# Fixed rings, a first sequence in halves, decays on C and their inverse on x, and weights that GpSimd's DMA queue casts on the way

## The chip, the cores and the metric

The kernel runs on one core of a Trainium2 chip. A core has TensorE (PE, matrix products), VectorE (DVE), ScalarE (ACT), GpSimd (POOL) and SyncE (SP), which all work from lists of instructions in order, and 16 DMA engines. Here only SyncE, ScalarE and GpSimd issue DMAs. The metric is the device time of one execution in microseconds: median 124.69 us of three runs (124.38 to 125.62) for the kernel before.

## The reference

A state-space scan (four batches called sequences here, eight heads, 768 steps, head dimension 32, state dimension 16) is followed by a two-layer network with a GELU on the 3072 tokens of 256 features. Cut to what matters:

```
log_a = log(clip(a, 1e-6, 1))
for each chunk c (32 steps here; any chunk length gives the same y):
    cum = cumsum(log_a[c])
    M   = (C_c B_c^T) * exp(cum_i - cum_j) * causal
    y_c = M x_c + (C_c state) * exp(cum_i)
    state = exp(sum log_a[c]) * state + B_c^T (x_c * exp(cum_last - cum_j))
x   = y as [tokens, heads * head_dim]           # 3072 x 256
out = gelu_tanh(x @ w_in) @ w_out               # w_in 256 x 2048, w_out 2048 x 256
```

All inputs and the output are float32. Both kernels keep products of decays instead of logarithms and multiply bf16 on TensorE.

## The kernel before

**Work.** Chunks of 128 steps: six per sequence, 24 in all, in units of one chunk (units 0 and 1) or two (units 2 to 12). For a unit, `f_G` makes the grams C B^T of all heads into the bank tile `gb` (L648), `f_M` masks them into `m` (L658, VectorE), `f_D` makes the state's increments (L669), `f_S` and `f_SP` update the state and spread it by head (L719, L726, VectorE), `f_Y` makes the output into `yb` (L691, L700), and `f_yev` copies it to `xm` (L709, ScalarE). Then the network: `f_s1` is a group of eight or four matmuls with w_in (L746) into one of two banks `hp`, `f_gelu` turns a bank into `gT` (L754, ScalarE, 96 times), `f_s2` is a group of four matmuls with w_out (L763) into one bank, and `f_oev` and `f_store` take a chunk out (L770, L772). The last chunk goes in two halves of columns (`f_s2h`, L781).

**Sequence preparation.** The decays' products run backwards through a chunk (`f_R`, `f_scang`); B is multiplied by them and C by their reciprocal, then both are transposed: chunk 0 by a path of its own (`f_mul0`, `f_T0`, `f_ce0`, `f_bh0`), the rest of sequence 0 by TensorE (`f_RT`, L481; `f_mul`, L584; `f_T`, L593; `f_E`; `f_F`, L608), sequences 1 to 3 on VectorE (`f_mulg`, L522; `f_Tg`, L532; `f_Fg`, L542). B in its plain layout, which `f_D` needs, comes by transposing back on TensorE (`f_N`, L614) and a copy on ScalarE (`f_bn`, L447). x is cast to bf16 by `f_castx` (L449 on GpSimd).

**Weights.** w_in and w_out come in four quarters each, as float32, through SyncE's queue (`load_wi` L439, `load_wo` L443) into tiles `wf`; `f_wi` and `f_wo` cast them into `w_in_sb` and `w_out_sb` (L449 GpSimd, L451 VectorE).

**Order.** Every step is a node with an engine, a duration, dependencies and a priority. `run_order` plays the nodes and emits them in the order of its own clock; the table `PRIO` holds the priorities. The loads take places in SyncE's list in the order in which the code names them: B and C, x, w_in, x, w_in, x, w_out, x, then the sequences. Where TensorE would be idle before the first `f_s2`, `idle` puts in matmuls on zeros (fillers, L1054).

Of the kernel before, what the change touches and what calls it, by code (L numbers as in the profile page):

```python
# [14 lines left out]
class Node:  # L15


    def __init__(self, eng, dur, fn, deps=(), prio=0.0, done=0.0):
        self.eng, self.dur, self.fn, self.prio, self.done = eng, dur, fn, prio, done
        self.deps = [d for d in deps if d is not None]  # L20
        self.allocs = []
        self.after = 0.0
        self.start = self.end = None

    def takes(self, pool, *by):

        self.allocs.append((pool, list(by)))
        return self


def run_order(nodes, pools, hop=0.08, same=0.04, idle=None, wait=()):

    hist = {p: [] for p in pools}
    free = {}
    todo = list(nodes)
    order = []

    def est(n):
        t = 0.0
        for d in n.deps:  # L40
            if d.end is None:
                return None
            t = max(t, d.end + n.after
                    + (d.done + hop if d.eng != n.eng else 0.0 if n.eng == "PE" else same))
        for pool, _ in n.allocs:
            h = hist[pool]
            if len(h) >= pools[pool]:
                for d in h[-pools[pool]]:
                    if d.end is None:
                        return None  # L50
                    t = max(t, d.end + (same if d.eng == n.eng else hop))
        return t

    while todo:
        best = None
        cand = {}
        for n in todo:
            e = est(n)
            if e is not None:
                cand.setdefault(n.eng, []).append((e, n))  # L60
        assert cand, [(n.eng, n.prio, n.fn) for n in todo[:5]]
        for eng, c in cand.items():
            t = max(free.get(eng, 0.0), min(e for e, _ in c))
            if best is None or t < best[0]:
                best = (t, eng)
        t, eng = best
        ready = [(n.prio, e, i, n) for i, (e, n) in enumerate(cand[eng]) if e <= t + 1e-9]
        ready.sort(key=lambda r: r[:3])
        n = ready[0][3]
        if eng in wait:  # L70
            soon = [(e, m) for e, m in cand[eng] if t < e < t + n.dur - 0.1 and m.prio < n.prio - 5]
            if soon:
                e1 = min(e for e, _ in soon)
                fit = [r[3] for r in ready if t + r[3].dur <= e1 + 0.1]
                if fit:
                    n = fit[0]
                else:
                    t, n = min(((e, m) for e, m in soon if e <= e1 + 0.1),
                               key=lambda r: r[1].prio)
        if idle is not None and eng == "PE":  # L80
            x = idle(free.get(eng, 0.0), t)
            if x is not None:
                order.append((free.get(eng, 0.0), x))
        n.start, n.end = t, t + n.dur
        free[eng] = n.end
        for pool, by in n.allocs:
            hist[pool].append(by)
        todo.remove(n)
        order.append((t, n.fn))
    return order  # L90
# [1001 lines left out]
```

## Time and profile before

| | |
|---|---|
| median of three runs | 124.69 us (124.38 to 125.62) |
| span of the profiled execution, first to last instruction | 122.2 us |
| what lies around the span (median less span) | 2.5 us |
| first `f_s1` group | starts 12.30 us |
| last cast of a w_out quarter | 24.86 us, 1.04 us long |
| last matmul's end | about 118.8 us |

The profile is of one execution; its own time outside of the profiler isn't shown, so its span is set beside the median of the runs. Busy shares of the page are averages over the whole span. A matmul's entry lasts longer than the slot it takes in the pipeline: groups of eight with 256 columns follow each other 0.87 us apart, 0.109 us each.

### The profile page before, as it was taken

What the parts mean: (1) busy time and instruction counts of PE and PEld (TensorE: products, weight loads), DVE (VectorE), ACT (ScalarE), POOL (GpSimd) and SP (SyncE); (2) the same over time, 40 slices, a digit from 0 to 9 for tenths busy, and PEclk for the clock granted to TensorE, in tenths of its full rate; (3) what the DMA queues carried; (4) which work ended last, traced back from release to release, by engine and by line L of the source; (5) the groups of instructions that cost most, each with busy time, mean ns of one, the idle gap of its engine ahead of it and who ended that gap; (6) DMA issues with size and microseconds to landing.
All of it is one profiled execution on the core that took longest, in us unless ns stands there. A gap on an engine that the chain in (4) does not pass through costs nothing.

```text
span 122.2 us, 3518 instructions
## 1 busy us (share of the span) xinstructions
PE 112.5 (92%) x1484; PEld 98.9 (81%) x1484; DVE 69.7 (57%) x161; ACT 75.8 (62%) x145; POOL 18.7 (15%) x38
## 2 busy tenths in 40 slices
PE   5899969999999999779997799999999999999980
PEld 5788658788988898678986679989898899999970
DVE  3887888929979997961959549065656300000100
ACT  4024836775765877468675566768677867767710
POOL 7304565560050005003200000000000000000000
PEclk9999999999999999999999999999999999999999
DMA  2999939979958796598011010111011001111111
GB/s 51 255 267 244 343 106 353 326 163 192 201 151 217 141 222 167 148 197 205 6 43 43 5 43 0 48 46 43 5 43 43 27 21 43 43 48 43 38 48 43
DMA packets 44250, 14.27 MB, mean 117 GB/s; under 512 B 39052, under 2 KB 42700, under 8 KB 44236
## 3 DMA queue, kind: packets, MB, share of 16 engines
q1 hardware_dynamic: 43148, 13.95, 46.1%
q10 hardware_dynamic: 1088, 0.11, 0.7%
q8 instruction: 11, 0.18, 0.6%
q14 instruction: 3, 0.02, 0.1%
HBM read 10.91 MB, written 3.15 MB: 115 GB/s over the span
## 4 chain that ended last, share of the span: by engine, by line
PE 73%; SPq 13%; DMA 5%; ACT 4%; issue 1%; POOL 1%; DVE 0%; ACTq 0%; DVEq 0%
PE hp L746 31%; PE o_ps L763 30%; SPq L431 5%; DMA wf<-in_moe_w_out_dram 5%; SPq L443 4%; PE yb L763 3%; ACT gT L754 2%; PE gb L648 2%; SPq L439 2%; PE yb L700 2%; PE yb L691 2%; PE gb L781 1%; SPq L315 1%; ACT o_sb L770 1%; POOL w_out_sb L449 1%
## 5 line engine op out<-in xcount | busy, mean ns | idle before, releaser
L754 ACT ACTIVATE gT<-hp 128x512 bf16<-128x512 f32 x96 | 54.1, 596 | 24.9 <-PE hp L746 24.7
L746 PE MATMUL hp<-xm,w_in_sb 128*128 128x256 bf16 (+1 forms) x416 | 53.6, 267 | 4.0 <-ACT gT L754 2.7
L746 PEld LDWEIGHTS <-w_in_sb 128*128 128x128 bf16 x416 | 42.0, 115 | 7.9 <-issue 5.7
L763 PE MATMUL o_ps<-w_out_sb,gT 128*128 128x256 bf16 x336 | 44.4, 273 | 0.5 <-POOL w_out_sb L449 0.5
L763 PEld LDWEIGHTS <-gT 128*128 128x128 bf16 x368 | 35.7, 98 | 4.3 <-issue 0.7
L658 DVE TENSOR_TENSOR m<-gb,tri 128x1024 bf16<-128x1024 f32 (+1 forms) x25 | 28.5, 1174 | 1.0 <-PE gb L648 1.0
L772 DVE COPY o_sb<-o_ps 128x256 f32<-128x256 f32 x1 | 0.4, 424 | 18.6 <-ACT gT L754 18.6
L770 ACT ACTIVATE o_sb<-o_ps 128x256 f32<-128x256 f32 x20 | 7.7, 385 | 5.0 <-ACT gT L754 2.6
L719 DVE SCALAR_TENSOR_TENSOR s_new<-s_new,pend,hp 128x64 f32<-128x64 f32 x16 | 4.5, 279 | 11.0 <-PE hp L669 10.8
L726 DVE SCALAR_TENSOR_TENSOR sp_new<-s_new,pend,bmask 128x256 bf16<-128x256 f32 x20 | 10.2, 521 | 0.3
L1054 PE MATMUL o_ps<-wz 128*128 128x128 bf16 x75 | 8.9, 281 | 1.3 <-DVE warm L353 1.3
L449 POOL CAST x<-xs_t 128x512 bf16<-128x512 f32 x9 | 5.4, 635 | 26.5 <-DMA xs_t<-in_x_dram 17.3
L709 ACT ACTIVATE xm<-yb 128x512 bf16<-128x512 f32 (+1 forms) x13 | 7.3, 563 | 2.3 <-PE yb L700 2.1
L1054 PEld LDWEIGHTS <-wz 128*128 128x128 bf16 x75 | 6.9, 129 | 1.6 <-DVE warm L353 1.3
L700 PE MATMUL yb<-m,x 128*32 128x128 bf16 x192 | 6.3, 223 | 0.0
L449 POOL CAST w_in_sb<-wf 128x512 bf16<-128x512 f32 x6 | 4.3, 728 | 8.9 <-DMA wf<-in_moe_w_in_dram 8.9
L691 PE MATMUL yb<-ce,sp_new 128*32 128x128 bf16 x160 | 5.3, 221 | 0.0
L648 PE MATMUL gb<-ce,bh 32*128 32x256 bf16 x96 | 5.1, 278 | 0.0
L717 DVE COPY s_new<-hp 128x64 f32<-128x64 f32 x4 | 0.9, 221 | 7.0 <-PE hp L669 7.0
L449 POOL CAST w_out_sb<-wf 128x1024 bf16<-128x1024 f32 x4 | 4.2, 1041 | 3.0 <-DMA wf<-in_moe_w_out_dram 3.0
L700 PEld LDWEIGHTS <-x 128*32 128x32 bf16 x192 | 3.8, 97 | 0.8 <-issue 0.8
L691 PEld LDWEIGHTS <-sp_new 128*32 128x32 bf16 x160 | 2.9, 96 | 1.7 <-issue 1.6
(83 smaller groups left out, 69.5 us busy)
## 6 DMA issues: line engine op xcount, KB each, us to landing
out_dram<-o_sb SPq DMA_DIRECT2D x23, 128.0 KB, 1.7
xs_t<-in_x_dram SPq DMA_DIRECT2D x3, 768.0 KB, 5.9
wf<-in_moe_w_in_dram SPq DMA_DIRECT2D x4, 512.0 KB, 8.8
wf<-in_moe_w_out_dram SPq DMA_DIRECT2D x4, 512.0 KB, 6.9
bc_t<-in_B_dram SPq DMA_DIRECT2D x12, 96.0 KB, 3.1
bc_t<-in_C_dram SPq DMA_DIRECT2D x12, 96.0 KB, 2.3
x_t<-in_x_dram SPq DMA_DIRECT2D x6, 128.0 KB, 7.3
bc_t<-in_C_dram SPq DMA_DIRECT2D x1, 384.0 KB
```

What stands on the lines that cost most here:

```text
L449: nc.gpsimd.tensor_copy(out=o, in_=i)
L648: nc.tensor.matmul(out=gb[:, g, 256 * k:256 * k + 256], lhsT=bh_of(gc)[32 * g:32 * g + 32], rhs=ce_of(gc)[32 * g:32 * g + 32], start=True, ...
L658: nc.vector.tensor_tensor(out=MT[gc][:, g0:g1], in0=gb[:, g0:g1, 256 * k:256 * k + 256] .rearrange("p g (e t) -> p g e t", e=2), in1=tri_b ...
L691: nc.tensor.matmul(out=y4[32 * j:32 * j + 32, k, w], lhsT=sp[:, 32 * h:32 * h + 32], rhs=ce_of(gc)[:, h % 2], start=first(j), stop=False, ...
L700: nc.tensor.matmul(out=y4[32 * j:32 * j + 32, k, w], lhsT=X16[u][:, k, 32 * h:32 * h + 32], rhs=m[:, h // 2, h % 2, :], start=first(j), st ...
L709: nc.scalar.activation(xm[:, :, t0:t0 + n * Q].rearrange("p w (c t) -> p c w t", c=n), y4[:, 0:n], AF.Copy)
L726: nc.vector.scalar_tensor_tensor(out=sp_new.rearrange("p (g d) -> p g d", g=4), in0=state[("s", gc)].rearrange("p (o d) -> p o d", o=1).to ...
L746: nc.tensor.matmul(out=hp[:, j * nt:(j + 1) * nt], lhsT=w_in5[:, kc, fi // 4, fi % 4], rhs=xm[:, kc, t0:t0 + nt], start=(kc == 0), stop=(k ...
L754: nc.scalar.activation(gts[u][:, i * per:(i + 1) * per, 0:nt], hps.pop((u, i)).rearrange("p (j t) -> p j t", j=per), AF.Gelu_apprx_tanh)
L763: nc.tensor.matmul(out=ops[gc], lhsT=gts[u][:, fi, tt * Q:(tt + 1) * Q], rhs=w_out_sb[:, fi, :], start=(fi == 0), stop=(fi == NF - 1), ski ...
L770: nc.scalar.activation(o_sb, ops.pop(gc), AF.Copy)
L1054: nc.tensor.matmul(out=zb[:, 0:128], lhsT=wz[:, 0:128], rhs=wz[:, 0:128], start=True, stop=True)
```

## The change

The scheduler with its nodes and priorities goes. In its place stands a string `ORDER` of 630 words, each a step with its arguments, which is played from the front; it sets each engine's list. Tile pools become single tiles and rings that hand out their buffers in turn. The beginning of the string, which covers the steps up to chunk 0's `f_s2`:

```
c,wz c,cz c,idf c,tri c,ident lbc,0,0,SP la,1,ACT la,3,ACT la,0,SP la,2,ACT c,first c,selp c,aone
bz,0,0,3,DVE lbc,0,1,SP lbc,1,0,SP clip lbc,1,1,SP c,warm bz,0,3,6,POOL lx,0,SP dwi,0 lx,1,SP scan
z,19,g T,0,2 E,0,2,0,43,ACT z,5,g N,0,1 E,0,2,43,64,ACT bn,0,1,ACT p6 cz,0,1 lx,3,SP lx,2,SP pt,0
N,1,3 bn,1,3,ACT bz,1,3,6,ACT pt,2 cz,0,0 T,0,1 E,0,1,0,43,ACT inv,0,0,1 cz,1,1 cz,1,0 c,m16
bz,1,0,3,POOL e2,0 e2,1 T,0,0 E,0,0,0,43,ACT c,bmask pp E,0,1,43,64,ACT asp G,0 E,0,0,43,64,DVE
M,0,0,0,2 M,0,0,2,4 T,1,0 E,1,0,0,64,ACT pend xs,0,POOL T,1,1 E,1,1,0,64,ACT dwi,1 pt,1 inv,0,1,6
T,1,2 D,0 G,1 Y,0 E,1,2,0,64,ACT yev,0 xs,1,POOL z,2,o N,3,6 bn,3,6,ACT S,0,0 M,1,0,0,4 s1,0,0 SP,0
D,1 dwi,2 G,2 S,1,0 xs,2,POOL Y,1 ge,0,0 pk dwi,3 dwo,0 dwo,1 z,11,o s1,0,1 dwo,2 dwo,3 ge,0,1
...
```

`dwi` and `dwo` are the weights, `xs` the scaling of x, `s1`, `ge` and `s2` the network, `z` fillers, `lbn` and `cbn` B in its plain layout, `l...` loads. What else changes:

- **Weights**: one DMA for each quarter, issued by GpSimd, from float32 in memory into the bf16 tile. No cast instruction is left.
- **Decays**: the products run forwards (`f_scan`, `f_scang`); C is multiplied by them, B is only cast, and x is multiplied by their inverse (`f_inv`, `f_xs`) where it was only cast before. The sign of heads is put in by two zero-filled tiles `cz` for sequence 0.
- **Sequence 0** comes in two halves of 384 steps on 64 partitions each; chunk 0 has no path of its own any more. The end-of-chunk decays go through GpSimd (`f_e2`, `f_pend`).
- **Sequences 1 to 3**: B in its plain layout is loaded a second time, 64 bytes at a time (`f_lbn`), and cast on GpSimd (`f_cbn`); the transposing back and its copy go. B's cast is on GpSimd too (`f_cB`). Their loads have buffers of their own.
- **Outputs**: seven whole chunks are taken out by VectorE instead of one.
- Gram, increment and output of a unit are single steps, where before they went as one from unit 5 on. There are five `gT` buffers, six before.

```diff
-    def load_wi(q):
-        WF[("i", q)] = wfp.tile([128, 2, 512], FP32, name="wf")
-        nc.sync.dma_start(out=WF[("i", q)], in_=wi[:, :, q * 512:(q + 1) * 512])
...
-    def f_wi(q, k0, k1, eng):
-        for k in range(k0, k1):
-            copy(eng, w_in_sb[:, k, q * 512:(q + 1) * 512], WF[("i", q)][:, k])
...
+    def f_dwi(q):
+        nc.gpsimd.dma_start(out=w_in_sb[:, :, q * 512:(q + 1) * 512], in_=wi[:, :, q * 512:(q + 1) * 512])
+
+    def f_dwo(q):
+        nc.gpsimd.dma_start(out=w_out_sb[:, 4 * q:4 * q + 4], in_=wo[q])
...
+    def f_lbn(b, q):
+        queue[q].dma_start(out=bnf[b], in_=bass.AP(
+            tensor=B.tensor, offset=B.offset + b * H * S * N, ap=[[N, Q], [Q * N, H * CPB], [1, N]]))
...
+    def f_inv(b, c0, c1):
+        js = slice(H * b, H * b + H)
+        nc.vector.reciprocal(invp[:, c0:c1, js], (pk if b else ptok)[:, c0:c1, js])
...
+    def f_cz(half, e):
+        s = slice(64 * half, 64 * half + 64)
+        nc.vector.tensor_tensor(
+            out=cz[e][s].rearrange("p r (g e) n -> p e r g n", e=2)[:, e],
+            in0=bc0[s, 1].rearrange("p (g e) (r n) -> p e r g n", e=2, n=N)[:, e],
+            in1=p6[s, :, 0:H].rearrange("p r (g e o) -> p e r g o", e=2, o=1)[:, e]
+            .to_broadcast([64, R6, 4, N]), op=ALU.mult)
...
+    def f_cbn(b, eng):
+        copy(eng, bn[b].rearrange("p c (h n) -> p c h n", n=N),
+             bnf[b].rearrange("p (h c) n -> p c h n", c=CPB))
...
+    def f_xs(u, eng):
+        n = len(UNITS[u])
+        X16[u] = x16.take()
+        b, c = divmod(UNITS[u][0], CPB)
+        o = X16[u][:, 0:n].rearrange("p c (h d) -> p c h d", h=H)
+        w = invp[:, c:c + n, H * b:H * b + H].rearrange("p c (h o) -> p c h o", o=1)
+        if b:
+            ttt(eng, o, xs[b].rearrange("p (h c) d -> p c h d", c=CPB)[:, c:c + n],
+                w.to_broadcast([128, n, H, D]))
+        else:
+            for k in range(n):
+                ttt(eng, o[:, k], XT[c + k], w[:, k].to_broadcast([128, H, D]))
...
+    steps = {k[2:]: f for k, f in locals().items() if k.startswith("f_")}
+    for word in ORDER.split():
+        name, *args = word.split(",")
+        steps[name](*(int(v) if v.isdigit() else v for v in args))
```

More of the change, by code (lines that the diff above doesn't have):

```diff
@@ L10 @@
 BF16 = mybir.dt.bfloat16
+I32 = mybir.dt.int32
 AF = mybir.ActivationFunctionType
 ALU = mybir.AluOpType
[L15 to L28, printed above, removed]
@@ L31, in run_order @@
[L31 to L90, printed above, removed]
@@ L251, with __init__, take @@
+s1,12,7 ge,12,6 s2,12,0,1,y ge,12,7 s2,12,0,2,y s2,12,0,3,y s2h,0 s2h,1 oev,21,ACT oev,22,DVE
+oevh,0,DVE st,22 sth,0 st,21 oevh,1,ACT sth,1
+"""
+class Ring:
+    def __init__(self, bufs):
+        self.bufs, self.n = bufs, 0
+    def take(self):
+        self.n += 1
+        return self.bufs[(self.n - 1) % len(self.bufs)]
 @with_exitstack
@@ new lines @@
+    a_t = sb("a_t", [128, 256])
+    ac = sb("ac", [128, 256])
+    p_t = sb("p_t", [128, 256])
+    first = sb("first", [128, 256])
+    p6 = sb("p6", [128, R6, BH])
+    pk = sb("pk", [128, CPB, BH])
+    invp = sb("invp", [128, CPB, BH])
+    e2 = sb("e2", [128, 2, batch, 2, 3])
+    asp = sb("asp", [128, 2, batch, CPB])
+    pend = sb("pend", [128, batch, CPB])
+    ptok = ob[:, 0:CPB * BH].rearrange("p (c j) -> p c j", c=CPB)
+    ptok3 = ob[:, 0:CPB * BH].rearrange("p (k l j) -> p k l j", k=2, l=3)
@@ new lines @@
+    warm = sb("warm", [128, 1])
+    idf = sb("idf", [128, 128])
+    ident = sb("ident", [128, 128], BF16)
+    bmask = sb("bmask", [128, H * D], BF16)
+    tri = sb("tri", [128, Q], BF16)
+    tri_b = tri.rearrange("p (o q t) -> p o q t", o=1, q=1).to_broadcast([128, 4, 2, Q])
+    sel8 = sb("sel8", [128, H])
+    selp = sb("selp", [128, H, N])
+    m16 = sb("m16", [128, 16])
+    par = sb("par", [128, 2])
+    pari = sb("pari", [128, 2], I32)
+    zeros = wz.bitcast(FP32)
+    XT, X16, MT, DT, ST, SP, GT, HP, OP, OS, PT = ({} for _ in range(11))
@@ L451, in copy, with ttt @@
             nc.vector.tensor_copy(out=o, in_=i)
-    def f_wi(q, k0, k1, eng):
-        for k in range(k0, k1):
-            copy(eng, w_in_sb[:, k, q * 512:(q + 1) * 512], WF[("i", q)][:, k])
-    def f_wo(q, eng):
-        copy(eng, w_out_sb[:, 4 * q:4 * q + 4], WF[("o", q)])
-    def f_clip(i0, i1):
-        nc.vector.tensor_scalar(out=ac[:, i0:i1], in0=a_t[:, i0:i1], scalar1=1e-6, scalar2=1.0,
+    def ttt(eng, o, i0, i1, op=ALU.mult):
+        (nc.gpsimd if eng == "POOL" else nc.vector).tensor_tensor(out=o, in0=i0, in1=i1, op=op)
@@ new lines, with f_la, f_lbc @@
+    queue = {"SP": nc.sync, "ACT": nc.scalar, "POOL": nc.gpsimd}
+    def f_la(k, q):
+        t0 = 192 * k - 64 * (k % 2)
+        c0, n = (0, 256) if k % 2 else (64, 192)
+        queue[q].dma_start(out=a_t[32 * k:32 * k + 32, c0:c0 + n], in_=bass.AP(
+            tensor=a.tensor, offset=a.offset + t0, ap=[[S, BH], [1, n]]))
+    def f_lbc(i, half, q):
+        src = (B, C)[i]
+        queue[q].dma_start(
+            out=bc0[64 * half:64 * half + 64, i],
+            in_=bass.AP(tensor=src.tensor, offset=src.offset + half * HS * N,
+                        ap=[[R6 * N, 64], [S * N, H], [1, R6 * N]]))
@@ L485, in f_recip0, with f_p6, f_pt @@
-    def f_recip0():
-        nc.vector.reciprocal(q0, rp0)
-    def f_recip():
-        nc.vector.reciprocal(pt, RP[1])
+    def f_p6():
+        nc.vector.transpose(out=p6, in_=p_t[:, 64:256].rearrange("q (p r) -> q r p", r=R6))
+    def f_pt(l):
+        k, off = (0, 64) if l == 0 else (1, 128 * (l - 1))
+        nc.tensor.matmul(out=ptok3[:, :, l], lhsT=p_t[:, off:off + Q],
+                         rhs=idf.rearrange("p (k o j) -> p o k j", k=2, o=2)[:, k],
+                         start=True, stop=True, skip_group_check=True)
@@ new lines, in f_pp, with f_asp, f_pend @@
+    def f_pp():
+        nc.tensor.matmul(out=pps, lhsT=selp.rearrange("p h n -> p (h n)"),
+                         rhs=e2.rearrange("p t b k l -> p (t b k l)"), start=True, stop=True,
+                         skip_group_check=True)
+    def f_asp():
+        nc.scalar.activation(asp.rearrange("p t b c -> p (t b c)"), pps, AF.Copy)
+    def f_pend():
+        nc.gpsimd.tensor_tensor(out=pend[:, :, 0:CPB - 1], in0=asp[:, 1, :, 0:CPB - 1],
+                                in1=asp[:, 0, :, 1:CPB], op=ALU.mult)
@@ new lines, in f_T, with f_E @@
+    def f_T(half, w):
+        s = slice(64 * half, 64 * half + 64)
+        src = bz if w == 2 else cz[w]
+        t = yb if (half == 0 and w == 0) else hp.take()
+        PT[(half, w)] = t[:, 0:HS // 2].bitcast(BF16)
+        for r in range(R6):
+            nc.tensor.transpose(out=PT[(half, w)][:, r * 64:(r + 1) * 64],
+                                in_=src[s, r].rearrange("p h n -> p (h n)"), identity=ident[s, s])
+    def f_E(half, w, p0, p1, eng):
+        o = bh[0] if w == 2 else ce[0][:, w]
+        copy(eng, o[:, HS * half:HS * half + HS].rearrange("q (p r) -> q p r", r=R6)[:, p0:p1],
+             PT[(half, w)].rearrange("q (r p) -> q p r", r=R6)[:, p0:p1])
@@ L491, in f_clipg, with f_N, f_bn @@
+    def f_N(c0, c1):
+        PT[("n", c0)] = hp.take()[:, 0:HS].bitcast(BF16)
+        for c in range(c0, c1):
+            nc.tensor.transpose(out=PT[("n", c0)][:, c * Q:(c + 1) * Q],
+                                in_=bh[0][:, c * Q:(c + 1) * Q], identity=ident)
+    def f_bn(c0, c1, eng):
+        copy(eng, bn[0][:, c0:c1].rearrange("p c n -> p (c n)"), PT[("n", c0)][:, c0 * Q:c1 * Q])
     def f_clipg(b):
-        nc.vector.tensor_scalar(out=ac3[b], in0=at[b], scalar1=1e-6, scalar2=1.0,
+        nc.vector.tensor_scalar(out=at[b], in0=at[b], scalar1=1e-6, scalar2=1.0,
@@ L553, in f_pp @@
-    def f_pp():
-        RP[2] = psh.tile([128, 512], FP32, name="hp")
-        nc.tensor.matmul(out=RP[2][:, 0:NCH], lhsT=selp.rearrange("p h n -> p (h n)"),
-                         rhs=pe2.rearrange("p j c -> p (j c)"), start=True, stop=True,
-                         skip_group_check=True)
-    def f_pend():
-        nc.scalar.activation(pend.rearrange("p (b i c) -> p i b c", b=batch, i=2),
-                             RP[2][:, 0:NCH].rearrange("p (i b c) -> p i b c", b=batch, i=2), AF.Copy)
@@ L611, in f_N @@
-    def f_N(b):
-        U[b]["n"] = (gb[:, 1] if b else psh.tile([128, 512], FP32, name="hp"))[:, 0:S // 2].bitcast(BF16)
-        for c in range(1 if b == 0 else 0, CPB):
-            nc.tensor.transpose(out=U[b]["n"][:, c * 128:(c + 1) * 128],
-                                in_=U[b]["bh"][:, c * Q:(c + 1) * Q], identity=ident)
-    def f_bn(b, eng):
-        d = U[b]
-        d["bn"] = work.tile([128, CPB, 128], BF16, name="bn")
-        c0 = 1 if b == 0 else 0
-        copy(eng, d["bn"][:, c0:].rearrange("p c n -> p (c n)"), d["n"][:, c0 * 128:])
@@ L656, in f_M @@
         if g0 == 0:
-            MT[gc] = msb.tile([128, 4, 2, Q], BF16, name="m")
+            MT[gc] = mr.take()
         nc.vector.tensor_tensor(out=MT[gc][:, g0:g1],
@@ L738, in f_s1 @@
         per = 512 // nt
-        if u not in gts:
-            gts[u] = gpool.tile([128, NF, 256], BF16, name="gT")
-        hp = psh.tile([128, 512], FP32, name="hp")
-        hps[(u, i)] = hp
+        if u not in GT:
+            GT[u] = gtr.take()
+        HP[(u, i)] = hp.take()
         for j in range(per):
@@ L767, in f_oev, with f_st @@
     def f_oev(gc, eng):
-        o_sb = opool.tile([128, d_model], FP32, name="o_sb")
-        if eng == "ACT":
-            nc.scalar.activation(o_sb, ops.pop(gc), AF.Copy)
-        else:
-            nc.vector.tensor_copy(out=o_sb, in_=ops.pop(gc))
-        outs[gc] = o_sb
-    def f_store(gc):
-        nc.sync.dma_start(out=out[gc * Q:(gc + 1) * Q, :], in_=outs.pop(gc))
+        OS[gc] = orr.take()
+        copy(eng, OS[gc], OP[gc])
+    def f_st(gc):
+        nc.sync.dma_start(out=out[gc * Q:(gc + 1) * Q, :], in_=OS[gc])
     def f_s2h(h):
         for f in range(NF):
-            nc.tensor.matmul(out=gb[:, 2 * h, 0:128], lhsT=gts[NU - 1][:, f, Q:2 * Q],
+            nc.tensor.matmul(out=gb[:, 2 * h, 0:128], lhsT=GT[NU - 1][:, f, Q:2 * Q],
                              rhs=w_out_sb[:, f, 128 * h:128 * h + 128], start=(f == 0),
@@ L785, in f_oevh, with f_sth @@
     def f_oevh(h, eng):
[L786 to L789 removed]
+        OS[("h", h)] = orr.take()
+        copy(eng, OS[("h", h)][:, 0:128], gb[:, 2 * h, 0:128])
+    def f_sth(h):
         nc.sync.dma_start(out=out[(NCH - 1) * Q:NCH * Q, 128 * h:128 * h + 128],
[L791 to L803 removed]
@@ L1036 @@
-    for u in range(MERGE, NU):
-        Yn[u].deps.append(gpn[(u - 2, 0)])
-    for u in range(GT_BUFS, NU):
-        gpn[(u, 0)].deps.append(oevn[UNITS[u - GT_BUFS][-1]])
-    for n in nodes:
-        n.prio = PRIO.get(n.name, n.prio)
-    zb = pso.tile([128, 512], FP32, name="o_ps")
-    def idle(t0, t1):
-        t0 = max(t0, 1.25)
-        n = int((t1 - t0 - 0.05) / (0.107 if t0 < 6.3 else 0.2 if 9.5 < t0 < 13.2 else 0.07))
-        if s2_first[0].start is not None or n < 1:
-            return None
-        def fill():
-            for _ in range(n):
-                nc.tensor.matmul(out=zb[:, 0:128], lhsT=wz[:, 0:128], rhs=wz[:, 0:128],
-                                 start=True, stop=True)
-        return fill
@@ L1058, with f_z @@
-    pools = {"hp": 2, "o": 1, "gram": 1, "yb": 1, "wf": 6, "ob": 6}
-    order = run_order(nodes, pools, idle=idle, wait=("DVE", "POOL"))
-    for t, fn in order:
-        fn()
+                          in_=OS[("h", h)][:, 0:128])
+    def f_z(n, bank):
+        t = gb[:, 3] if bank == "g" else ob
+        for _ in range(n):
+            nc.tensor.matmul(out=t[:, 384:512], lhsT=wz[:, 0:128], rhs=wz[:, 0:128],
+                             start=True, stop=True)
+    steps = {k[2:]: f for k, f in locals().items() if k.startswith("f_")}
```

757 lines of the change are left out of this document (256 added, 501 removed), and 152 rows, old and new, of the table PRIO.

## The prediction

> **What bounds the kernel now.** I read the page first (busy time, slices, chain), then busy time by stretch, then the order of time of the first 26 us, then the rows of the tile `wf`.
>
> ```profile
> span 122.2 us, 3518 instructions
> PE 112.5 (92%) x1484; PEld 98.9 (81%) x1484; DVE 69.7 (57%) x161; ACT 75.8 (62%) x145; POOL 18.7 (15%) x38
> PE 73%; SPq 13%; DMA 5%; ACT 4%; issue 1%; POOL 1%; DVE 0%; ACTq 0%; DVEq 0%
> ```
>
> TensorE (PE) is 73% of the chain that ended last; the 13% of SyncE's queue and the 5% of DMA all lie at its start. Busy time by stretch (columns: length, then busy us and count of PE, PEld, DVE, ACT, POOL, clock, DMA share, GB/s) shows where PE is not full:
>
> ```profile
> 16.00:20.00 4.00, 3.21 (x60) 3.07 (x60) 3.65 (x6) 1.91 (x5) 2.50 (x4) 1.00 0.61 229
> 24.68:49.00 24.32, 24.32 (x328) 21.06 (x328) 19.41 (x49) 16.88 (x33) 5.32 (x8) 1.00 0.90 183
> 49.00:53.00 4.00, 2.63 (x23) 2.22 (x22) 3.90 (x12) 2.18 (x4) 0.00 (x0) 1.00 0.68 151
> 65.00:72.00 7.00, 5.50 (x83) 4.43 (x80) 4.11 (x11) 4.26 (x9) 0.00 (x0) 1.00 0.09 30
> 72.00:118.80 46.80, 46.74 (x582) 42.61 (x574) 15.09 (x26) 31.96 (x62) 0.00 (x0) 1.00 0.11 37
> ```
>
> From 24.68 on PE is full but for two short stretches; the chain has 4.2 us on ScalarE (ACT) there (0.61+0.39+0.61 near 50, 0.38+0.61+0.61+0.39+0.61 from 65 to 72), where one bank waits to be emptied. So the kernel is a **ramp** up to about 25 us and a **full PE** after it. The order of time shows the ramp:
>
> ```profile
> 1.25 2.74 PE L1054 MATMUL o_ps<-wz 128*128 128x128 bf16 x24 [1.25 <-DVE warm L353]
> ...
> 9.71 1.33 POOL L449 CAST w_in_sb<-wf 128x512 bf16<-128x512 f32 x2 [5.52 <-DMA wf<-in_moe_w_in_dram]
> ...
> 12.30 0.95 PE L746 MATMUL hp<-xm,w_in_sb 128*128 128x128 bf16 x8
> ...
> 13.94 0.61 PE L746 MATMUL hp<-xm,w_in_sb 128*128 128x128 bf16 x8
> ...
> 24.68 0.60 PE L763 MATMUL o_ps<-w_out_sb,gT 128*128 128x256 bf16 x4 [0.51 <-POOL w_out_sb L449]
> ...
> 25.98 0.60 PE L763 MATMUL o_ps<-w_out_sb,gT 128*128 128x256 bf16 x4
> ```
>
> The first w_in quarter is cast at 9.71, the first `f_s1` group (L746) runs at 12.30, and the third and fourth quarters of w_out let chunk 0's last two `f_s2` groups (L763) go at 24.68 and 25.98. I take 25.98 as the **marker**: by then 12 `f_s1` groups are done (64 matmuls of 128 columns, 16 of 256), and 118.76-25.98 = 92.8 us of PE follow. Before it PE runs fillers (L1054).
>
> **The change, part by part.**
>
> *Weights.* Eight cast pieces go from GpSimd (4.3 + 4.2 us in the costliest groups) and two from VectorE (0.9). On GpSimd all of that was hidden except where it was last, at 24.68. In exchange the eight loads stand in GpSimd's own order, and they stand late: the second after the scaling of x for chunk 0, the third after chunk 1's, the fourth after chunks 2 and 3's. The changed program's list of instructions with their waits shows more. The first `f_s1` group's second weight load waits for the second w_in transfer, though it needs the first alone; the third w_in transfer waits for that group's last matmul; the second `f_s1` group waits for the third and the fourth transfer. (A transfer now writes both halves of `w_in_sb` at once, where each cast wrote one; the dependence is kept for the whole span between.) So there is a loop: transfer 2, `f_s1` group 1, transfer 3, x scaling, transfer 4, `f_s1` group 2. I follow it:
> - GpSimd up to transfer 2. Constants until 2.3 (like before's 1.69, with a wider `idf` and `tri` moved ahead). The copy of B's first half waits for its load: issued at 0.80, before's rows for B and C of the same tensors land after 3.2 to 4.8 us, the lower as the queues are empty: 4.0. Copy 0.6 (CAST 128x256 0.585). Issue 1. `m16` 0.12+0.18+0.26. Second copy 0.6: 6.8. Four tiny multiplications at 0.2: 7.6. `bmask` 0.31+0.45+0.45: 8.9. `pend` 0.2: 9.1. x scaling 0.65 (no two-input row of GpSimd; 0.585 is a one-input cast of that size): **issue of transfer 2 at 9.8**.
> - A GpSimd DMA issue isn't in this trace. SyncE's issues took 0.36 to 1.64 us when not stuck in a queue; I take 1.0, keep 0.4 to 1.6.
> - Landing. The only row for such a load is
>
> ```profile
> DMA to landing us min/median/max: 4.2/7.0/9.4
> ```
>
> and lower still by the 1.7 us of a 128 KB store, plus 1.3 us for the other 384 KB at 300 GB/s: 3.0. I take 5.0, near the row's minimum, since the weights have a queue of their own but share the 16 engines with x, B, C and sequence 1's loads, which SyncE can now issue at once (no buffer holds them back); both ends, 3.0 and 7.0, are kept.
> - Transfer 2 lands 14.8; group 1 done 15.6; transfer 3 issued 15.6 to 16.6; two x scalings 1.3: 17.9; transfer 4 lands **22.9**, when group 2 starts (before: 13.94). The w_out loads are issued right behind and land by 27, ahead of their use.
> - From there to the marker the new order has 10 `f_s1` groups, 3 of `f_s2`, the grams and outputs of unit 2. PE: 13 x 0.437 + 1.06 + 12 fillers at 0.055 = 7.4; the gelus at 0.60 with two banks: 6.6 with one eviction. PE decides: 7.4. But PE stood almost idle from about 11 to 22.9, and this trace has a half-speed state: 24 fillers at 114 ns each at 1.25, eight L746 in 0.95 at 12.30 and the same eight in 0.61 at 13.94 (about 0.10 and 0.055 apiece), with the clock row at 1.00 all along. I count 3.3 us of wall time at half speed: +1.6. Marker at 22.9 + 9.0 = **31.9**: +5.9 us, with one `f_s1` group still to do (+0.44).
>
> The Trainium skill (TensorE: Matmul & The Clock Gate, Part 1) has that as a gate: PE idle for a window of about 3.4 us falls to half rate and needs about as much activity to come back. The trace agrees with the two rates, not with the clock row. By that rule the sum is the one above; without it 1.6 less.
>
> The Trainium skill (DMA: Bandwidth & Descriptors, Anatomy of one DMA) gives a GpSimd load 2.0 us + bytes/436e3, an estimate of 3.2 us here. Taken twice for my 5.0, the time would be 127.4.
>
> *First sequence in halves; decays on C, inverse on x.* The 24 fp32 matmuls of L481 (1.53 us) become three; masking by VectorE of ce (L608, 1.5 us) goes, since C is multiplied into two zero-filled tiles. Chunk 0's special path (gram at 6.66, output at 9.96) is replaced by half-sequence transposes: scan of 256 columns (0.7), transposition, two multiplications of 384 (0.55 each), copies on ACT at 0.39; its gram comes at about 8.2, its output at about 10.4. That is 0.4 us late, and hidden behind the wait for transfer 2.
>
> *B's columns by DMA.* The 18 transposes of L614 go from PE (chain pieces 0.33+0.34+0.34: **-1.0**), and ACT's three evictions of 0.81. Instead 6144 pieces of 64 bytes per sequence are loaded, at most as long as the x load of equally many pieces (5.9 us); sequence 1 is wanted near 40, so that is covered unless DMA is still 10 us behind, in which case it is paid in full.
>
> *Full-PE stretch.* Six more output evictions go to VectorE (0.42 each), some x scalings too (0.7). ACT loses 2.4 + 6 x 0.385 us, so up to 4.2 us of its waits may go. But VectorE's queue is longer: between `f_D(3)` and the gram of unit 4 it has S, SP, `par`, clip, scan, transpose, Tg, two multiplications, Tg, two masks: 0.28+0.52+0.55+0.22+0.42+0.44+0.36+0.73+0.38+0.69 = 4.6 us after one M of 1.2, and PE has only nine groups and one output, 4.5: it waits about 1.3 there, and something under 1 before most later grams. I take **+1.0** net, ends -4.2 and +4.
>
> *Sum* on the span: 122.2 + 5.9 + 0.44 - 1.0 + 1.0 = 128.5. The median of three runs (124.69) lies 2.5 above the profiled span; I keep these 2.5: **131.0 us**.
>
> **Rivals.**
> - *Weights in time (faster).* If GpSimd's loads issue in 0.4 and land in 3.0, transfer 2 lands at 12.2, group 1 ends 12.9, transfer 4 is issued at 14.6 and lands 17.6. With warm PE the marker is at 25.0; with ACT's 4.2 gone too the span is 122.2-1.0+0.44-1.0-4.2 = 116.4, time 118.9; with half of them gone 121. It decides once transfer 4 lands before 18.6. For it: an own queue past SyncE's stalls (4.02 us at 12.73). Against: the loop leaves PE idle twice whatever the speed. Chance 0.07.
> - *It cancels*, within 1%: landing near 4.2 with a warm PE, ramp +2, stretch -1.5: 124 to 126. Chance 0.08.
> - *Quick landings*: landing 3.0, all else as in the sum: transfer 2 lands 12.8, group 1 ends 13.6, transfer 4 is issued 15.9 and lands 18.9, marker 27.9, time 127.0. For it: the weights' large pieces against x's small ones on each engine. Chance 0.20. (The Trainium skill's 3.2 above points here.)
> - *Forecast*: the loop holds at landings of 4.2 to 6: 128.5 to 134. Chance 0.52.
> - *Slower still*: SyncE's many small pieces take the engines while GpSimd's loads wait (landing 7.0, issue 1.6): transfer 2 lands 17.4, transfer 4 28.1, marker 37: +11+0.44-1+3, time 138. Chance 0.13. (The Trainium skill, SBUF — State Buffer, SBUF: two separate sides, says that VectorE's copies in a two-port mode keep GpSimd from writing descriptors; no run here shows it yet, and it would lead here.)
> - *No gain because a cast remains*: the new program has none on any engine, so no chance is given.
>
> **Numbers.** Range 126 to 137: quick landings and the forecast whole, half of what is slower still; the first two cases are left out. One per cent, 1.2 us, is about what three runs can tell (they span 124.38 to 125.62). Faster 0.07, within 1% 0.08, slower 0.85.
>
> **What would show it.** Right: GpSimd's second DMA issue near 10; PE idle or on fillers from 11 to 15 and from 17 to 22; the second `f_s1` group waiting for a w_in transfer; half-speed matmuls after it; marker near 32; PE's share below 90%; PE waiting for VectorE before unit 4's gram. Wrong: `f_s1` groups running at 13 to 18, GpSimd's loads landing within 3 us, or stalls in the full-PE stretch shrinking by 4 us.

## The result, and the profile after

The changed kernel takes 134.19 us (median of four runs, 133.63 to 134.98), the kernel before 124.53 beside it: 1.0754 times as long (95% interval 1.0681 to 1.0826). The profile's page, with the lines that answer to those shown of before:

```profile
span 133.2 us, 3460 instructions
PE 112.8 (85%) x1443; PEld 97.1 (73%) x1443; DVE 70.3 (53%) x156; ACT 72.2 (54%) x142; POOL 27.5 (21%) x50
PE 67%; DMA 13%; DVE 6%; POOL 6%; issue 4%; ACT 1%; DVEq 0%; POOLq 0%
```

TensorE is as busy as before in microseconds (112.8 against 112.5), but the span is 11.0 longer. 13% of the chain is now DMA. Where, the chain in order of time says (start, length, what), from B's first load to the fourth `f_s2` group of chunk 0, the prediction's marker:

```profile
10.37 0.52 POOL x L211
10.89 6.37 DMA w_in_sb<-in_moe_w_in_dram
...
17.30 0.94 PE hp L584 x7
18.24 0.20 PE hp L510 x3
...
18.54 0.76 POOL w_in_sb L243
...
19.32 1.14 POOL x L211 x2
20.45 8.00 DMA w_in_sb<-in_moe_w_in_dram
...
28.59 0.91 PE hp L584 x7
```

This is the loop, link by link: transfer 2 (issued 10.89), group 1 of `f_s1` (L584), the matmuls right behind it (L510) whose end lets transfer 3 be issued, x's scaling, transfer 4, group 2. Busy time by stretch (length, then busy us and count of PE, PEld, DVE, ACT, POOL, clock, DMA share, GB/s) shows what TensorE did meanwhile (a DMA share above 1 means that the times of packets overlapped):

```profile
11.00:20.00 9.00, 5.04 (x71) 3.22 (x71) 3.87 (x7) 2.42 (x6) 2.71 (x5) 1.00 0.98 158
20.00:28.60 8.60, 0.90 (x10) 0.67 (x8) 1.36 (x2) 0.00 (x0) 4.48 (x8) 1.00 1.28 151
28.60:38.10 9.50, 9.48 (x139) 8.06 (x140) 2.49 (x5) 5.91 (x11) 0.83 (x1) 1.00 1.13 154
38.10:51.00 12.90, 12.90 (x156) 10.96 (x155) 11.27 (x32) 8.14 (x16) 0.00 (x0) 1.00 0.48 103
```

From 20.0 to 28.6 TensorE, VectorE and ScalarE are nearly idle; GpSimd's 4.48 us are scalings, issues and casts, all done by 24.5. The order of time on TensorE gives the marker, 38.12 (before: 25.98), and the half rate that follows the wait: eight matmuls of 128 columns in 1.04 us at 30.96, in 0.61 at 34.15.

```profile
30.96 1.04 PE L584 MATMUL hp<-xm,w_in_sb 128*128 128x128 bf16 x8
...
34.15 0.61 PE L584 MATMUL hp<-xm,w_in_sb 128*128 128x128 bf16 x8
...
38.12 0.60 PE L601 MATMUL ob<-w_out_sb,gT 128*128 128x256 bf16 x4
```

So the ramp is 12.1 us longer. From the marker to the start of the last 32 matmuls (L781 before, L614 after) it is 90.82 us before and 89.41 after: there the change gains 1.4. The rest of the 11.0 is 0.3 at the end.

In the table, "ramp" is the marker and "rest" the time from it to the start of those last matmuls; the ratio is to the kernel before, measured beside each. The profiles of the fillers' run and of the one with loads held until the last issue come from executions somewhat longer than the others of the same kernel; their ramps are read from them, their times from the ratio, and their rests are left out.

| run | ramp | rest | ratio, 95% interval |
|---|---|---|---|
| before | 25.98 | 90.82 | 1 |
| changed | 38.12 | 89.41 | 1.0754 (1.0681 to 1.0826) |
| four w_in tiles | 27.74 | 91.44 | 1.0193 (1.0149 to 1.0237) |
| SyncE held until transfer 4 landed | 34.58 | 91.78 | 1.0735 (1.0674 to 1.0795) |
| the same, w_out later | 33.99 | 93.06 | one run, 134.47 us |
| loads issued early, one tile | 28.59 | 90.20 | 1.0181 (1.0108 to 1.0254) |
| 101 fillers | 35.97 | - | 1.0566 (1.0482 to 1.0651) |
| weights cast as before | 27.61 | 93.97 | 1.0344 (1.0265 to 1.0422) |
| four tiles, x scaled later | 27.62 | 89.21 | 1.0117 (1.0040 to 1.0194) |
| the same, SyncE held to the last issue | 26.95 | - | 1.0266 (1.0211 to 1.0322) |
| four tiles, x scaled later, loads early | 27.97 | 89.26 | 0.9972 (0.9943 to 1.0002) |

### The profile page after: what moved, and what is told of

It reads as the page before. It is cut to its first block, busy times and chain, and to the rows that moved or that the text cites. A ratio compares the mean times of both kernels' runs of the same rounds, so it can differ in the third digit from the quotient of the medians.

```text
span 133.2 us, 3460 instructions
## 1 busy us (share of the span) xinstructions
PE 112.8 (85%) x1443; PEld 97.1 (73%) x1443; DVE 70.3 (53%) x156; ACT 72.2 (54%) x142; POOL 27.5 (21%) x50
## 4 chain that ended last, share of the span: by engine, by line
PE 67%; DMA 13%; DVE 6%; POOL 6%; issue 4%; ACT 1%; DVEq 0%; POOLq 0%
PE hp L584 30%; PE ob L601 26%; DMA w_in_sb<-in_moe_w_in_dram 11%; DMA bc<-in_B_dram 3%; PE gb L490 2%; PE yb L601 2%; PE yb L532 2%; PE yb L540 2%; DVE sp L567 2%; POOL x L211 1%; POOL w_in_sb L243 1%; PE hp L510 1%; PE ob L629 1%; DVE m L498 1%; POOL bz L206 1%
## 5 line engine op out<-in xcount | busy, mean ns | idle before, releaser
L584 PE MATMUL hp<-xm,w_in_sb 128*128 128x256 bf16 (+1 forms) x416 | 54.7, 270 | 11.9 <-DMA w_in_sb<-in_moe_w_in_dram 11.7
L584 PEld LDWEIGHTS <-w_in_sb 128*128 128x128 bf16 x416 | 43.0, 115 | 14.9 <-issue 9.0
L601 PE MATMUL ob<-w_out_sb,gT 128*128 128x256 bf16 x336 | 46.4, 273 | 0.3 <-DVE o_sb L208 0.2
L560 DVE SCALAR_TENSOR_TENSOR s<-s,pend,hp 128x64 f32<-128x64 f32 x16 | 4.4, 272 | 13.6 <-PE hp L510 13.0
L567 DVE SCALAR_TENSOR_TENSOR sp<-s,pend,bmask 128x256 bf16<-128x256 f32 x20 | 10.7, 546 | 0.1
L204 ACT ACTIVATE o_sb<-ob 128x256 f32<-128x256 f32 x16 | 6.2, 385 | 7.1 <-issue 3.8
L211 POOL TENSOR_TENSOR x<-wf,invp 128x512 bf16<-128x512 f32 x5 | 5.8, 1180 | 17.9 <-DVE invp L346 17.9
L629 PEld LDWEIGHTS <-wz 128*128 128x128 bf16 x49 | 4.7, 137 | 1.9 <-DVE wz L273 1.3
L532 PE MATMUL yb<-ce,sp 128*32 128x128 bf16 x160 | 5.6, 230 | 0.1
L532 PEld LDWEIGHTS <-sp 128*32 128x32 bf16 x160 | 2.9, 99 | 2.4 <-issue 1.4
L243 POOL DMA_DIRECT2D w_in_sb<-in_moe_w_in_dram x4 | 3.2, 796 | 6.1 <-PE hp L510 6.1
L601 PE MATMUL yb<-w_out_sb,gT 128*128 128x256 bf16 x32 | 4.3, 272 | 0.0
```

The lines of the kernel that those rows point to most:

```text
L204: nc.scalar.activation(o, i, AF.Copy)
L211: (nc.gpsimd if eng == "POOL" else nc.vector).tensor_tensor(out=o, in0=i0, in1=i1, op=op)
L532: nc.tensor.matmul(out=y4[32 * j:32 * j + 32, k, w], lhsT=SP[gc - 1][:, 32 * h:32 * h + 32], rhs=ce[b][:, h % 2, cs], start=begins(j), sto ...
L567: nc.vector.scalar_tensor_tensor(out=SP[gc].rearrange("p (g d) -> p g d", g=4), in0=ST[gc].rearrange("p (o d) -> p o d", o=1).to_broadcast ...
L584: nc.tensor.matmul(out=HP[(u, i)][:, j * nt:(j + 1) * nt], lhsT=w_in5[:, kc, fi // 4, fi % 4], rhs=xm[:, kc, t0:t0 + nt], start=(kc == 0), ...
L601: nc.tensor.matmul(out=OP[gc], lhsT=GT[u][:, fi, tt * Q:(tt + 1) * Q], rhs=w_out_sb[:, fi, :], start=(fi == 0), stop=(fi == NF - 1), skip_ ...
```

## The experiments

**Is it the shared span of `w_in_sb`, or the place of the issues?** Two runs on the changed kernel. In the first, w_in stands in four tiles, so that no transfer's span takes in another quarter; every engine's order stays.

```diff
-    w_in_sb = sb("w_in_sb", [128, 2, d_ff], BF16)
+    w_in_q = [sb(f"w_in_q{q}", [128, 2, 512], BF16) for q in range(4)]
...
-        nc.gpsimd.dma_start(out=w_in_sb[:, :, q * 512:(q + 1) * 512], in_=wi[:, :, q * 512:(q + 1) * 512])
+        nc.gpsimd.dma_start(out=w_in_q[q], in_=wi[:, :, q * 512:(q + 1) * 512])
...
-                                 lhsT=w_in5[:, kc, fi // 4, fi % 4],
+                                 lhsT=w_in5[fi // 4][:, kc, fi % 4],
```

> w_in is kept in four tiles, one per quarter; the order of every engine and the eight loads stay as they are in the changed kernel (marker 38.1 us, span 133.2). Theory of the loop: the waits of group 1 on transfer 2, of transfer 3 on group 1 and of group 2 on transfers 3 and 4 go. Group 1 then starts with its first matmul near 13.1, transfer 3 is issued near 12.5 and transfer 4 near 14.5, group 2 (quarter 1) starts near 17.3, group 4 near 21, and the last w_out quarter lands by 27: marker 26 to 28.5, time 122.5 to 125. Rival, only the late issue and the slow landings count: transfer 4 lands where it did within 2 us, marker 36 to 38, time 132 to 134.

TensorE's order of time in that run:

```profile
12.72 1.02 PE L584 MATMUL hp<-xm,w_in_q 128*128 128x128 bf16 x8
...
16.13 0.98 PE L584 MATMUL hp<-xm,w_in_q 128*128 128x128 bf16 x8
...
19.10 0.64 PE L584 MATMUL hp<-xm,w_in_q 128*128 128x128 bf16 x8 [1.05 <-DMA w_in_q<-in_moe_w_in_dram]
...
21.38 1.08 PE L584 MATMUL hp<-xm,w_in_q 128*128 128x128 bf16 x16 [0.86 <-DMA w_in_q<-in_moe_w_in_dram]
...
27.74 0.60 PE L601 MATMUL ob<-w_out_sb,gT 128*128 128x256 bf16 x4 [0.76 <-DMA w_out_sb<-in_moe_w_out_dram]
```

Group 1 starts at 12.72, group 2 at 16.13, groups 3 and 4 wait about 1 us each for their quarters, and the marker waits 0.76 for the last of w_out: 27.74, 10.4 us earlier, with the same eight loads on the same queue. So 10.4 of the ramp's 12.1 us were the loop's waits and what followed from them. The time, 126.63 us, is 1.6 over the upper end expected, because the rest grew by 2.0 (below).

In the second, the single tile stays and the loads move forward on GpSimd (here and below, of a line of `ORDER` only the words around the change are shown):

```diff
-c,warm bz,0,3,6,POOL lx,0,SP dwi,0 lx,1,SP scan
+c,warm dwi,0 dwi,1 bz,0,3,6,POOL lx,0,SP dwi,2 lx,1,SP scan
...
-bz,1,0,3,POOL e2,0
+bz,1,0,3,POOL dwi,3 e2,0
```

(and `dwo,0` to `dwo,3` behind `xs,0` and `xs,1`.)

> The changed kernel with the eight loads earlier in GpSimd's order and w_in in one tile as it was: transfers 1 and 2 ahead of the copy of B's first half (where GpSimd stood idle from 2.4 to 4.3), transfer 3 behind it, transfer 4 behind the copy of B's second half, the w_out loads behind the scaling of chunk 0 and of chunk 1. Theory: the false waits stay, but all four transfers are issued by 8 us and land by 15, so that they cost at most 2 us: group 1 at 13.5 to 15.5, marker 27 to 30, time 123 to 126. Rival, the shared span alone decides (the loop keeps its shape wherever the loads are issued): marker beyond 34. Rival, weights ahead of x and B take their DMA share: the first output and with it group 1 come 2 us later than 15.5, marker above 30.

Ramp 28.59; 126.17 us, 0.2 over the upper end expected. So the dependence on the shared span costs little when all four transfers are issued before it bites: it was the dependence and the place together that made the loop. The third theory showed in part: the first `f_s1` group starts at 16.42, against 12.72 with four tiles, though the marker stays below the 30 that it named. The chain there holds a load of C that took 7.97 us (issued 3.59), where the two loads of C took 4.3 (median) in the changed kernel. The weights, now ahead of C, share the DMA engines with it; the later start was made up because no later group waited for a transfer.

**Why did the transfers take 6.4 and 8.0 us?** SyncE's later loads are held by a copy of one element per partition that itself waits for transfer 4:

```diff
+    def f_hold():
+        nc.gpsimd.tensor_copy(out=xt.bufs[4][:, 0, 0:1], in_=w_in_sb[:, 1, d_ff - 1:d_ff])
...
-pk dwi,3 dwo,0 dwo,1 z,11,o s1,0,1 dwo,2 dwo,3 ge,0,1
+pk dwi,3 dwo,0 dwo,1 z,11,o s1,0,1 dwo,2 dwo,3 hold ge,0,1
```

> The changed kernel with one GpSimd copy of one element (from the last column of w_in into the buffer of x's fifth chunk) behind the last w_out issue, so that SyncE's loads from x's fifth chunk on (sequence 1 among them) wait until transfer 4 has landed. It tells why transfers 2 and 4 took 6.4 and 8.0 us. Contention with SyncE's many pieces: they take 3 to 4.5 us, transfer 4 lands near 22, marker 30 to 32.5; sequence 1's data come some 5 us later than they did against the marker, so part of that gain is lost near the first gram of sequence 1. Rival, the landing is the GpSimd queue's own: 6 to 8 us as before, marker 37 to 39. Second rival, VectorE's copies hold the descriptors up: transfer 2, in whose flight VectorE is busy, stays near 6, transfer 4 too.

The chain of that run, and under it DMA by queue (packets, MB, share of the 16 engines' time) in the flight of transfer 4, in the changed kernel (20.4 to 28.5) and here (17.9 to 24.2):

```profile
10.54 4.23 DMA w_in_sb<-in_moe_w_in_dram
...
17.98 6.22 DMA w_in_sb<-in_moe_w_in_dram
```

```profile
q0 software_dynamic: 760, 0.93, 77.9%
q1 hardware_dynamic: 4701, 0.30, 52.3%
```

```profile
q0 software_dynamic: 709, 0.86, 96.5%
```

Transfer 2 went from 6.4 to 4.2 us, transfer 4 from 8.0 to 6.2: SyncE's many pieces were 2.2 and 1.8 us of them. In the flight of transfer 4 they were 4701 pieces of 64 bytes. Transfer 2 fell into the first theory's 3 to 4.5 us, transfer 4 did not, and the marker, 34.58, lies between the ranges of the two theories. In transfer 4's flight here GpSimd's queue (q0) alone takes 96.5% of the engines' time. That left its own transfers, so the next run held the w_out loads back as well (`hold` ahead of `dwo,0`).

> The run with SyncE's loads held until transfer 4 has landed, and the four w_out loads held until then as well (GpSimd's copy that waits for transfer 4 stands ahead of them). There transfer 4 took 6.2 us with only GpSimd's own transfers in flight: the third w_in load, issued 1.9 us earlier, and the four of w_out right behind. Theory that the four w_out loads share the engines with it: 4.0 to 4.7 us, like transfer 2's 4.2. Rival, a load of GpSimd's behind another one waits for it in the queue: 5.7 to 6.5 us as before.

Transfer 4 took 5.05 us, between the two theories: of its 8.0 us, 1.8 were SyncE's pieces and 1.2 the four w_out loads. The 5.05 that are left lie 0.4 to 0.8 over transfer 2's 4.2 to 4.6 in the held runs; that this goes with transfer 3, issued 1.9 us ahead, is argued from the difference alone.

VectorE's copies as a cause fall: VectorE was busy 2.69 us of transfer 2's 6.4 in the changed kernel and 2.75 us of its 4.2 here, and 1.4 of the 8.6 us around transfer 4, the slowest. Both held runs win at the marker and lose it: 133.55 us and 134.47. Sequence 1's data come late, and TensorE waits 2.4 us for VectorE's `ce` (the masked C that a gram needs) in the first of them.

**The half rate.** The fillers ahead of group 2 go from 11 to 101 (`z,101,o`).

> The changed kernel with 101 filler matmuls in place of 11 ahead of the second f_s1 group, so that TensorE works through most of its wait for transfer 4. Theory of the half speed: at 0.115 us for the first 30 and 0.055 after, they end near 27; the matmuls of group 2 at 28.6 run at full rate (eight in 0.61 instead of 0.91 to 1.04), marker 36.2 to 37.0, time 1.1 to 1.9 us less than the changed kernel's 134.2. Rival, the rate after the wait doesn't matter because ScalarE's gelus set the pace: marker 37.8 to 38.4, time 134.

```profile
19.69 7.00 PE L629 MATMUL ob<-wz 128*128 128x128 bf16 x101
...
28.03 0.56 PE L584 MATMUL hp<-xm,w_in_sb 128*128 128x128 bf16 x7 [1.28 <-DMA w_in_sb<-in_moe_w_in_dram]
```

Seven matmuls of group 2 take 0.56 us after the fillers, 0.91 without. From group 2's first of these to the marker it is 7.94 us against 9.53: the half rate cost 1.6 us, the prediction's term. (The marker came 2.15 earlier than in the changed kernel; the other 0.56 is an earlier landing of transfer 4, which took 7.2 us instead of 8.0.) The clock row says 1.00 in both.

**The weights' part undone alone.** SyncE loads the quarters in float32 and GpSimd and VectorE cast them, in the changed kernel's frame:

```diff
-lx,0,SP dwi,0 lx,1,SP scan
+lx,0,SP lwi,0,SP lwi,1,SP lx,1,SP lwi,2,SP lwi,3,SP scan
...
-xs,0,POOL T,1,1 E,1,1,0,64,ACT dwi,1 pt,1
+xs,0,POOL wi,0,0,POOL wi,0,1,POOL T,1,1 E,1,1,0,64,ACT wi,1,0,POOL wi,1,1,POOL pt,1
```

> The changed kernel with the weights' part alone undone: SyncE loads the quarters in fp32 (into the buffers that sequences 2 and 3 use later; w_in's behind x's first two chunks, w_out's behind its fourth), and GpSimd and VectorE cast them, each cast in one half of a quarter as in the kernel before. Theory that the loop of GpSimd's loads is the whole loss: the ramp is near the kernel before's again (marker 25.98), group 1 at 12.5 to 14, marker 26 to 29, time 122.5 to 126.5 (sequence 1's loads come behind the weights, which may cost 1 to 2 us near its first gram). Rival, the other parts (sequence in halves, decays on C, rings, order) cost the time: marker beyond 31 or, with a marker below 29, a time above 129.

Ramp 27.61, as expected; time 128.81, 2.3 over the upper end and just under the 129 that the rival named. Against the kernel before the ramp is 1.6 us longer and the rest 3.2; the run doesn't tell how much of it lies in the other parts and how much in the places that the loads and casts have in the new order. The chain there shows a load of x (one of the third and fourth chunks) landing 7.25 us after 10.13, and sequence 1's loads of B and C going out only from 20.0 to 29.1, behind the weights on SyncE (in the changed kernel 11.7 to 18.3). TensorE then waits 2.0 us for `ce` and 2.5 for ScalarE in the rest. So once the loop is gone the weights' own queue seems worth something: 126.63 with four tiles against 128.81. But the order of SyncE's loads and the casts differ too, and no run separates these.

**What grew in the rest of the four-tile run?** There TensorE waited 2.0 us for `ce` before unit 7's gram, the first of sequence 2. VectorE's order of time showed two multiplications of C (L440) in 2.06 us, elsewhere 0.64, while GpSimd scaled x for units 7 to 9. The run moves these scalings behind the copy of sequence 2's plain B (`cbn,2`):

```diff
-oev,5,ACT xs,8,POOL xs,9,POOL xs,7,POOL s1,4,0
+oev,5,ACT s1,4,0
...
-cbn,2,POOL s2,4,1,2,o
+cbn,2,POOL xs,7,POOL xs,8,POOL xs,9,POOL s2,4,1,2,o
```

> The kernel with four w_in tiles (126.6 us) and one move in GpSimd's order: the x scalings of units 7, 8 and 9 behind the copy of sequence 2's B. There GpSimd's three scalings ran from 50.6 to 53.9 and two VectorE multiplications of C took 2.06 us instead of 0.65 to 0.7, one masked state 0.97 instead of 0.48; TensorE then waited 2.0 us for VectorE before unit 7's gram. Theory that GpSimd's work slows VectorE's two-input work: the pair goes back to 0.65 to 0.8, the wait to 0.1 to 0.7, time 125.0 to 125.6. Rival, the multiplications waited for a load of sequence 2: the pair stays near 2, the wait near 2.0, time 126.4 to 127.

VectorE, four tiles first, then the moved scalings:

```profile
50.91 2.06 DVE L440 TENSOR_TENSOR bcw<-wf,at 128x192 bf16<-128x192 f32 x2
```

```profile
50.98 0.64 DVE L439 TENSOR_TENSOR bcw<-wf,at 128x192 bf16<-128x192 f32 x2
...
56.08 1.22 DVE L566 SCALAR_TENSOR_TENSOR sp<-s,pend,bmask 128x256 bf16<-128x256 f32 x1
```

The pair is back at 0.64, the waits for `ce` fell from 2.0 to 0.6 in all, the rest from 91.44 to 89.21, the time to 124.94. The loss moved with the scalings: they now run from 55.97 to 59.21, and the masked state at 56.08 takes 1.22 in place of 0.48, where nobody waits for it.

**A better one?** Two tries on top of that. One holds SyncE's loads from x's fifth chunk on until GpSimd has issued its last w_out load (a memset of one element per partition at 17.2).

> The same again, and SyncE's loads from x's fifth chunk on wait until GpSimd has issued its last w_out load (a one-element memset of that chunk's buffer behind it), near 17 us. If the many pieces of sequence 1 are what stretched w_in and w_out (6.6 and 9.5 us median, the last w_out load 11.3), group 3 starts near 17, group 4 near 19.5, the last w_out quarter lands by 24, marker 24.5 to 26, and sequence 1's data (cast at 28.2 and 34.1 before) come 3 to 5 us later, still ahead of its transposes: time 121.5 to 124, under the kernel before. If the weights' landing is their own queue's, marker 27 to 28 and time 125 to 126.5.

Ramp 26.95, 0.7 less, but the time is 127.54 us: 1.0266 times the kernel before where it was 1.0117. That is 1.9 us more, so the rest lost about 2.5. w_in's median landing went from 6.8 to 5.8 only, and sequence 1's C is multiplied near 34.9 (33.5 without the hold); TensorE waited 3.8 us for `ce` (0.6). Both theories missed: the hold buys the weights little, and sequence 1 has no such slack. The other moves the weights forward instead:

```diff
-bz,1,0,3,POOL e2,0 e2,1 T,0,0 E,0,0,0,43,ACT c,bmask pp
+bz,1,0,3,POOL dwi,1 e2,0 e2,1 T,0,0 E,0,0,0,43,ACT pp
...
-pend xs,0,POOL T,1,1 E,1,1,0,64,ACT dwi,1 pt,1
+pend xs,0,POOL dwi,2 c,bmask T,1,1 E,1,1,0,64,ACT pt,1
```

(with `dwi,3 dwo,0` behind `xs,1`.)

> The kernel with four w_in tiles and the later x scalings (124.9 us, marker 27.6, w_in's quarters in use at 12.9, 17.3, 19.8 and 21.6), with the loads earlier on GpSimd and the output mask's construction (1.2 us) moved behind the scaling of chunk 0: transfer 2 issued near 7 instead of 10.7, transfer 3 near 10.5, transfer 4 near 12.5, the last w_out load near 16 instead of 16.8. If issue places set the ramp: group 2 at 15.5 to 16.5, marker 25.3 to 26.7, time 122.8 to 124.2, level with the kernel before or a little under it. If the 16 DMA engines are the limit until then (any earlier load makes another late): marker 27 to 29, time 124.5 to 126.5.

Transfer 2 is issued at 6.97, 3.8 us earlier, and group 4 starts at 21.24 instead of 21.62; the last w_out load takes 10.6 us and the marker is 27.97. The marker is the second theory's: a load that goes earlier makes another late. That the 16 engines are the limit fits their share, between 1.09 and 1.34 from 5 to 28 us. The time, 124.11 us, is the first theory's (up to 124.2). It is 0.9972 times that of before (0.9943 to 1.0002): level with it, after three repairs. Why it is below the 124.94 of the run without this move stays open: the profiled executions (124.65 here, 124.24 there) have nearly the same rest, and the ramp here is 0.35 longer. No version here beats the kernel before by more than can be measured.

## Why the prediction came out as it did

The direction and the mechanism were right: the loop it followed from the list of waits is the chain of the profile after, and four tiles take it away. The time, 134.19, lies in the range (126 to 137), just above the end of the forecast (128.5 to 134) and below the 138 of "slower still"; it is 3.2 us over the 131.0 of the sum. Its steps:

| step | predicted | measured |
|---|---|---|
| transfer 2 issued | 9.8 | 10.89 |
| an issue on GpSimd | 1.0 (0.4 to 1.6) | 0.76 to 0.90 |
| landing | 5.0 twice (3.0 to 7.0) | 6.37 and 8.00 |
| group 2 starts | 22.9 | 28.59 |
| group 2 to the marker | 9.0, of which 1.6 half rate | 9.53, of which 1.6 |
| marker | 31.9 | 38.12 |
| marker to the last matmul, against before | +0.44 | -1.4 |
| around the span | 2.5 | 1.0 for the median, 1.8 for the profiled execution (134.98) |

- **The mis-sized term is the landing**: 4.4 of the 6.2 us by which the marker was late. I took a value near the minimum of the only row, "since the weights have a queue of their own", though the sentence goes on to the 16 shared engines. An own queue did not help there: SyncE's pieces cost 2.2 and 1.8 us of the two flights, and transfer 4 had its own queue's five other loads beside it. The upper bound of 7.0 was too low for the second flight. "Slower still" had priced two landings of 7.0, near the mean of 7.2.
- **Transfer 2 was 1.1 us late** mostly because the four tiny multiplications on GpSimd (L356, L361), costed at 0.2 each, took 0.64, 0.51, 0.23 and 0.55. The cost itself was right: in the run with the loads issued early they took 0.23, 0.20, 0.23 and 0.20. There VectorE stood idle from 6.3 to 9.8, waiting for C; in the changed kernel it multiplied C (`cz`, two inputs in SBUF) from 7.07 on. What the sum left out is this overlap. (By its own terms it gives 9.7: `bmask`'s 1.21 takes 7.6 to 8.8, not 8.9.) The first scaling of x took 0.61, costed at 0.65. The changed kernel first, then the early issue:

```profile
7.08 0.64 POOL L356 TENSOR_TENSOR e<-ac,m 128x16 f32<-128x16 f32 x1
...
8.35 0.55 POOL L361 TENSOR_TENSOR e<-p_t,m 128x8 f32<-128x8 f32 x1
```

```profile
7.40 0.23 POOL L356 TENSOR_TENSOR e<-ac,m 128x16 f32<-128x16 f32 x1
...
7.95 0.20 POOL L361 TENSOR_TENSOR e<-p_t,m 128x8 f32<-128x8 f32 x1
```

- **Half rate**: right to 0.1 us, as the fillers show, though it lasted 3.9 us where 3.3 were counted. The Trainium skill (TensorE: Matmul & The Clock Gate, Part 1) has an idle window and about as much activity to come back; after the 7.7 us wait the rate was half until about 32.5, 3.9 us, and after a wait of 1.28 us behind the fillers it stayed full. Both agree with it.
- **The estimate of 3.2 us** by the Trainium skill's formula for a load from GpSimd (DMA: Bandwidth & Descriptors, Anatomy of one DMA) was under every w_in load seen: 4.0 us was the least, in the run with SyncE held, and 4.2 for transfer 2 there, with SyncE's queue at 11.4% of the engines' time. The measurement decides; "quick landings" fell with it.
- **The rest** was forecast at +0.44 and came out at -1.4. TensorE's waits for ScalarE went, as at the far end of the forecast, but they weren't worth the 4.2 us priced there: those are the chain's pieces on ScalarE, while TensorE itself waited 2.7 us for it (line below). In the rest TensorE is idle for 1.9 us where it was 2.9, and works 0.4 less. The wait for VectorE before unit 4's gram (1.3 forecast) did not come; that TensorE's standstill had given VectorE a start is argued, not shown. With the ramp repaired it came three units later, before unit 7's, at 2.0; there GpSimd's scalings lengthened VectorE's work. The changed kernel itself shows 1.1 at that place. TensorE's waits, one line of before, then the changed kernel's:

```profile
PE hp L746 <- ACT gT L754: 2.7, 4, 0.7
```

```profile
PE gb L490 <- DVE ce L456: 1.1, 1, 1.1
PE hp L584 <- DVE s L560: 0.2, 1, 0.2
PE ob L601 <- DVE o_sb L208: 0.2, 1, 0.2
```

- **Transposes for loads**: B's 6144 pieces of 64 bytes per sequence were called covered. They were in the changed kernel, where no gram of sequence 1 waits. They weren't free: they are what shared the engines with transfer 4.
- **Around the span** 2.5 was 1.5 too much, which hid part of the miss: 6.2 - 1.8 + 0.3 - 1.5 = 3.2, the 134.2 against 131.0.

## What to carry to other kernels

When a load is moved to another queue, look first at what the program makes it wait for and who waits for it: here a transfer that writes two strided halves was held against everything between them, and a separate tile for each piece took 7.6 us off. Price a landing by the engines' busy share at that time, not by the queue being empty; with the 16 engines full, an earlier load made another late here. And judge a change in the steady part only once the ramp is repaired, since a long stall ahead hides what the engines behind it would cost.
